# A second double unit with seven block products, sums shared with GpSimd, and another opening list

## The chip, the cores and the metric

The kernel runs on one core of a Trainium2 chip. The metric is the device time of one execution in microseconds. TensorE (PE in the profile) multiplies, VectorE (DVE), ScalarE (ACT) and GpSimd (POOL) work on elements, SyncE (SP) only issues DMAs here, and POOL issues DMAs too.

## What is computed

The reference is a chunked attention followed by a two-layer block with a residual. Cut to what matters:

```python
# attention: 4 batches, 8 heads, 768 rows, 64 columns; 8 memory rows
for c in range(24):                       # chunks of 32 rows
    k_full = concat([mem_k, k[l_start:r_end]])   # 16 rows to the left, 8 to the right
    v_full = concat([mem_v, v[l_start:r_end]])
    scores = 0.125 * q_c @ k_full.T
    a = exp(scores - max(scores)); a = a / sum(a)
    out[c] = a @ v_full
# second block: x is out with the heads side by side, (4, 768, 512)
xn = (x - mean(x)) / sqrt(var(x) + 1e-6) * g_ln
out = x + relu(xn @ w_ch1) @ w_ch2        # 512 -> 2048 -> 512
```

Matmuls are in 16-bit floats with 32-bit sums; DMAs issued by POOL convert the 32-bit inputs on the way.

## The kernel before, in words

**Tiles.** The 3,072 rows are 24 token tiles t of 128 rows, six to a batch; two tiles make a unit u (0 to 11) of 256 rows. For a token tile: `qk_products` (L311) makes scores in one PSUM bank, `row_max` and `less_max` subtract the maximum on DVE, `weights` takes the exponential on ACT, `pt_products` and `pt_copy` turn the weights, `val_products` (L366) multiplies with V into the bank pair `two`, `tokens` (L380) divides and makes the negative mean on DVE, `shift` (L393) subtracts the mean on POOL or ACT, `x_products` and `x_copy` turn the tile and scale it by g, and `square` and `root_of` (L414, on POOL) make the reciprocal of the deviation, which `add_to` (L648) applies at the end.

**Up and down.** For units 0 to 9, `up_products(u, s, bank)` (L460) makes step s of 8 (256 of 2,048 hidden columns) with 8 matmuls 128x128 by 128x256, and `relu_up` evicts the bank. Down, for units 1 to 11, is a two-by-two block product (token halves by hidden halves by column halves) with seven products in place of eight, `down7_products(u, part, bank)` (L659), parts 0 to 6 of 8 matmuls each. Parts 2 to 6 add onto the bank of an earlier part, so an `add_to` on DVE must have read that bank first. The left sides of parts 2 to 5 are sums of relu blocks, `r_sum(u, k)` (L626, instruction at L637), k from 0 to 3: sum 1 uses sum 0, and sum 3 uses sum 1. A whole sum is 128x1024; with `lo, hi` it is made in halves of 128x512.

**Up with seven products.** Units 10 and 11 are one double unit: up is there a two-by-two block product too, of rows (unit 10, unit 11), x halves and hidden halves. `up7_products(c, k, bank, add)` (L558, matmuls at L578) makes product k (1 to 7) of a quarter c (0 to 3) with 4 matmuls. It needs sums of W1 blocks, `w1_sum(k, n, d, engine)` (L531, L542; 16 pieces of 128x512), and of x blocks, `x_sum(k, engine)` (L547, L554), called XS0 to XS3; XS1 uses XS0 and XS3 uses XS1. In one bank the products 1, 6, 5 and 3 are added up: after each of the first three, `hold` (L592) copies the bank to 32-bit floats on ACT, and after the last `relu_sum` evicts it on ACT. Products 2, 7 and 4 go to other banks, and `relu_of_sum` (L595, L596) on DVE adds a held copy and takes the relu.

**Banks.** Six PSUM banks are shared by all products: `one[0..1]`, `upb[0..1]`, `dnb[0..1]`.

**The order** is written out by hand, and each engine works through its own instructions in that order. There are three stretches. L707 to L1083 is the opening list: loads, units 0 to 2 and the attention of token tiles 0 to 9. From L1085 a plan spreads loads, attention and sums over 16 steps of each unit 3 to 7, between `up(u, step)` and `down7(u - 1, part)`. From L1149 on comes the tail, a list of units 8 to 11, down of unit 7 and the attention of tiles 18 to 23.

**The opening list.** POOL issues the loads in the order of the list: first two loads each of k, q, v of batch 0 in its first part and the same for its second part (12 loads, 2,304 KB in 16-bit), then `load_w1(0)`, `(2)`, `(1)`, `(3)` and `load_w2(0..3)` (512 KB each, L164, L169), with loads of batch 1 (`load_octets`, `load_v_group`) between. w1 chunk n holds the hidden columns of up steps 2n and 2n+1. The V tiles need ones behind each head: L713 writes them on DVE for both tiles at once. `mix` (L266) reorders loaded rows for the turns `turn_whole`, on DVE, ACT or POOL. The up steps of unit 0 come in the order 0, 5, 2, 4, 1, 3, 7, 6 (L841 on).

Of the kernel before, what the change touches and what calls it, by code (L numbers as in the profile page):

```python
# [18 lines left out]
def kernel(  # L19
# [31 lines left out]
    zeros = sb.tile([128, 512], FP16, name="zeros")  # L51
    mhalf = sb.tile([128, 1], FP32, name="mhalf")
# [443 lines left out]
    def down_add(t, p):  # L496
# [8 lines left out]
    flat_q = QD[0].rearrange("p j s -> p (j s)")  # L505
    RS_two = [
# [6 lines left out]
    rT_last = [  # L513
        raw[2][o].rearrange("p j r d -> p (j r d)").rearrange("p (n c) -> p n c", c=256)
        for o in range(2)
    ]
# [4 lines left out]
    XS = [P[0].rearrange("p (d c) -> p d c", d=2), P[1].rearrange("p (d c) -> p d c", d=2)] + [  # L521
        PT[i].rearrange("p j q -> p (j q)").rearrange("p (d c) -> p d c", d=2) for i in range(2)
# [5 lines left out]
    def r_totals(u):  # L528
        return RS_two if u == NP - 2 else RS
# [14 lines left out]
    def x_block(i, j):  # L544
        return xT[(NP - 2 + j) % 3][:, 2 * i : 2 * i + 2, :]

    def x_sum(k, engine):  # L547
        a, b = (
            (x_block(0, 1), x_block(0, 0)),
            (x_block(1, 1), XS[0]),  # L550
            (x_block(1, 1), x_block(0, 1)),
            (x_block(1, 0), XS[1]),
        )[k]
        on(engine).tensor_tensor(  # L554
            out=XS[k], in0=a, in1=b, op=ALU.subtract
        )

    def up7_products(c, k, p, add):  # L558
# [7 lines left out]
        def total(m):  # L566
# [6 lines left out]
            (block(0, 0), x_block(0, 0)), (block(1, 0), x_block(1, 0)), (total(3), x_block(1, 1)),  # L573
# [10 lines left out]
    def r_part(j, o, c):  # L584
        if j == 0:
            return rT[(NP - 2) % 2][:, 8 * o + 2 * c : 8 * o + 2 * c + 2, :]
        return rT_last[o][:, 2 * c : 2 * c + 2, :]
# [4 lines left out]
    def hold(p, e):  # L592
        nc.scalar.copy(out=e, in_=p)

    def relu_of_sum(j, o, c, p, e):  # L595
        nc.vector._custom_dve(  # L596
            TENSOR_ADD_SAT, out=r_part(j, o, c), in0=pair(p), in1=pair(e), s0=TOP, s1=0.0,
        )

    def relu_sum(c, p):  # L600
        nc.scalar.activation(out=r_part(1, 0, c), in_=pair(p), func=ACTF.Relu)
# [19 lines left out]
    def r_block(u, i, o):  # L621
        if u == NP - 1:
            return rT_last[o][:, :, 128 * i : 128 * i + 128]
        return rT[u % 2][:, 8 * o : 8 * o + 8, 128 * i : 128 * i + 128]

    def r_sum(u, k, lo=0, hi=8):  # L626
# [10 lines left out]
        nc.vector.tensor_tensor(  # L637
# [59 lines left out]

    VT = KT[1]
# [13 lines left out]
    for i in range(2):  # L712
        nc.vector.memset(V[i][:, :, :, 64:VW], 1.0)  # L713
        nc.vector.memset(V[i][0:16, 0, :, 64:VW] if i == 0 else V[i][0:16, 0, :, :], 0.0)
        nc.vector.memset(V[i][96:128, NG - 1, :, :], 0.0)
    nc.vector.memset(memv16[:, :, :, 64:VW], 1.0)
# [5 lines left out]
    copy_on("A")(out=mem16, in_=mem32)  # L722
    load_octets(0, 0, k, 0, 0, 48, (0,))
    load_octets(0, 0, k, 0, 0, 48, (1,))
    make_identity(nc, identity)
    mem_products(upb[1])
    warm(6, one[0])
    tk1 = turn(raw[0][0], 1, 48, one[0])
    load_octets(1, 0, q, 0, 0, 32, (1,))
    mem_copy(upb[1], "A")  # L730
    load_octets(1, 0, q, 0, 0, 32, (0,))
    mem_cols(VT, memT[:, 16:20, :], "V")
    tk0 = turn(raw[0][0], 0, 48, upb[0])
    warm(1, one[1])
    tq1 = turn(raw[1][0], 1, 32, one[1])
    to_rows(0, tq1, 1, "A", 32, 0, 16, 32)
    mem_cols(KT[0], memT[:, 0:4, :], "A")
    tq0 = turn(raw[1][0], 0, 32, dnb[1])
    to_rows(0, tq0, 0, "A", 32, 0, 16, 32)
    to_stream(KT[0], tk1, 1, "V", 48, 0)  # L740
    load_octets(2, 0, v, 0, 0, 48, (0,))
    to_stream(KT[0], tk0, 0, "V", 48, 0)
    warm(4, dnb[0])
    s1 = qk_products(1, dnb[0])
    to_rows(0, tq0, 0, "A", 32, 0, 0, 16)
# [12 lines left out]
    s0 = qk_products(0, upb[0])
    load_octets(2, 1, v, 0, 48, 48, (0,))
    load_octets(1, 1, q, 0, 32, 64, (1,))  # L760
    mix_into(whole[2], raw[2][1], 0, 96, "V")
    tV0 = turn_whole(whole[2], 0, 96, dnb[1])
    v1 = v_products(1, one[1])
    row_max(0, s0)
    less_max(0, s0)
    v_copy(1, v1, "V")
    v3 = v_products(3, upb[1])
    v0 = v_products(0, one[0])
    less_max(1, s1)
    v_copy(0, v0, "V")  # L770
    load_octets(0, 1, k, 0, 48, 48, (0,))
    load_octets(0, 1, k, 0, 48, 48, (1,))
    mix_into(whole[1], raw[0][1], 0, 96, "V")
    to_stream(VT, tV0, 0, "A", 48, 48)
    v_copy(3, v3, "A")
    v2 = v_products(2, upb[0])
    load_octets(1, 1, q, 0, 32, 64, (0,))
    load_w1(0)
    load_w1(2)
    load_w1(1)  # L780
    weights(0)
    load_w1(3)
    p0 = pt_products(0, dnb[1])
    weights(1)
    pt_copy(0, p0, "V")
    v_copy(2, v2, "V")
    p1 = pt_products(1, one[1])
    mix_into(whole[2], raw[2][1], 1, 96, "A")
    load_w2(0)
    val_products(0)  # L790
    tokens(0)
    mix_into(whole[3], raw[1][1], 1, 128, "A")
    tV1 = turn_whole(whole[2], 1, 96, upb[1])
    to_stream(VT, tV1, 1, "A", 48, 48)
    mix_into(whole[3], raw[1][1], 0, 128, "P")
    load_w2(1)
    tQ0 = turn_whole(whole[3], 0, 128, dnb[0])
# [4 lines left out]
    tQ1 = turn_whole(whole[3], 1, 128, one[0])  # L802
    to_rows(0, tQ0, 0, "A", 64, 32)
    pt_copy(1, p1, "V")
    val_products(1)
    load_octets(0, 0, k, 1, 0, 48, (0,))
    copy_on("V")(
# [3 lines left out]
    to_rows(0, tQ1, 1, "A", 64, 32)  # L811
    mix_into(whole[1], raw[0][1], 1, 96, "V")
    tK1 = turn_whole(whole[1], 1, 96, dnb[1])
    tokens(1)
    shift(0, "P")
    x0 = x_products(0, upb[0])
    x_copy(0, x0)
    to_stream(KT[0], tK1, 1, "V", 48, 48)
    shift(1, "A")
    tK0 = turn_whole(whole[1], 0, 96, one[1])  # L820
    to_stream(KT[0], tK0, 0, "A", 48, 48)
    load_octets(0, 0, k, 1, 0, 48, (1,))
    square(0)
    x1 = x_products(1, upb[1])
    load_v_group(1, 9, 1)
    x_copy(1, x1)
    v6 = v_products(6, dnb[0])
    v5 = v_products(5, one[0])
    square(1)
    v_copy(5, v5, "V")  # L830
    root_of(0)
    v4 = v_products(4, upb[0])
    v_copy(4, v4, "V")
    load_w2(2)
    load_w2(3)
    v10 = v_products(10, dnb[1])
    v_copy(10, v10, "V")
    s2 = qk_products(2, one[1])
    row_max(2, s2)
    load_mem_rows(1, B)  # L840
    up_products(0, 0, upb[1])  # L841
    relu_up(0, 0, upb[1], "V")
    up_products(0, 5, one[0])
    relu_up(0, 5, one[0], "A")
    load_v_group(1, 8, 1)
    less_max(2, s2)
    weights(2)
    load_v_group(1, 7, 1)
    load_octets(1, 0, q, 1, 0, 48, (0,))
    up_products(0, 2, upb[0])  # L850
    relu_up(0, 2, upb[0], "A")
    up_products(0, 4, dnb[1])
    relu_up(0, 4, dnb[1], "A")
    p2 = pt_products(2, upb[1])
    pt_copy(2, p2, "V")
    up_products(0, 1, one[1])
    relu_up(0, 1, one[1], "A")
    load_octets(0, 1, k, 1, 48, 48, (1,))
    v7 = v_products(7, one[0])
    v_copy(7, v7, "A")  # L860
    s3 = qk_products(3, upb[0])
    row_max(3, s3)
    less_max(3, s3)
    v8 = v_products(8, dnb[1])
    load_octets(0, 1, k, 1, 48, 48, (0,))
    v9 = v_products(9, upb[1])
    v_copy(9, v9, "A")
    val_products(2)
    tokens(2)
    shift(2, "P")  # L870
    mix(0, 0, "P")
    up_products(0, 3, one[1])
    relu_up(0, 3, one[1], "V")
    load_v_group(1, 1, 0)
    v_copy(6, v6, "V")
    w2_sum(0)
    weights(3)
    up_products(0, 7, one[0])
    up_products(0, 6, upb[1])
    relu_up(0, 6, upb[1], "A")  # L880
    load_octets(1, 0, q, 1, 0, 48, (1,))
    down_products(0, 0, upb[0])
    down_products(0, 1, upb[0])
    p3 = pt_products(3, one[1])
    down_products(1, 0, dnb[0])
# [576 lines left out]
```

## Time and profile before

| what | value |
|---|---|
| median of 3 runs | 224.45 us (224.44 to 224.99) |
| the profiled execution's own time | 224.56 us |
| its span, first to last instruction | 222.8 us |
| mean granted TensorE clock | 0.992 |
| bytes moved by DMA | 23.24 MB |

The profile's time is counted from the start of the span. "L637" is a line of the kernel. A line of a timeline gives the start, the duration, the engine, the line, the operation, out<-in and the form; in square brackets stand idle time of the engine just before it and what ended it. PEld is the weight load, which runs beside PE. A matmul is pipelined, so its shown duration overlaps the next one's.

### The profile page before, as it was taken

What the parts mean: (1) busy time and instruction counts of PE and PEld (TensorE: products, weight loads), DVE (VectorE), ACT (ScalarE), POOL (GpSimd) and SP (SyncE); (2) the same over time, 40 slices, a digit from 0 to 9 for tenths busy, and PEclk for the clock granted to TensorE, in tenths of its full rate; (3) what the DMA queues carried; (4) which work ended last, traced back from release to release, by engine and by line L of the source; (5) the groups of instructions that cost most, each with busy time, mean ns of one, the idle gap of its engine ahead of it and who ended that gap; (6) DMA issues with size and microseconds to landing.
All of it is one profiled execution on the core that took longest, in us unless ns stands there. A gap on an engine that the chain in (4) does not pass through costs nothing.

```text
span 222.8 us, 8324 instructions
## 1 busy us (share of the span) xinstructions
PE 213.6 (96%) x3578; PEld 188.3 (84%) x3578; DVE 178.3 (80%) x396; ACT 132.0 (59%) x260; POOL 128.2 (58%) x203
## 2 busy tenths in 40 slices
PE   6977999998999999999999999999999999999993
PEld 2456895698999989999999999999898999999982
DVE  6587956897898987896686996895789987788983
ACT  3297766677786388468447278378757743654100
POOL 7937327888989726976454937415277548930000
PEclk9996999999999999999999999999999999999999
DMA  4999999999984993994952992952100011101115
GB/s 76 183 191 207 213 205 208 189 136 133 137 52 57 206 162 68 130 74 113 157 73 57 144 131 59 107 98 63 50 3 3 3 47 50 47 4 49 47 56 184
DMA packets 43450, 23.24 MB, mean 104 GB/s; under 512 B 30004, under 2 KB 39796, under 8 KB 43364
## 3 DMA queue, kind: packets, MB, share of 16 engines
q0 software_dynamic: 38416, 14.48, 56.8%
q1 hardware_dynamic: 4996, 8.22, 12.7%
q8 instruction: 28, 0.46, 0.8%
q14 instruction: 10, 0.08, 0.1%
HBM read 29.02 MB, written 6.29 MB: 158 GB/s over the span
## 4 chain that ended last, share of the span: by engine, by line
PE 85%; DMA 4%; POOL 4%; DVE 3%; issue 1%; ACT 1%; DVEq 0%; POOLq 0%
PE upb L464 22%; PE dnb L643 20%; PE one L464 6%; PE one L643 5%; DMA raw<-in_q_dram 4%; PE upb L643 4%; PE two L373 4%; PE one L274 3%; POOL raw L107 3%; PE dnb L464 2%; PE dnb L578 2%; PE one L578 2%; PE one L429 2%; PE one L322 2%; PE dnb L490 2%; PE upb L490 2%
## 5 line engine op out<-in xcount | busy, mean ns | idle before, releaser
L464 PEld LDWEIGHTS <-w1c 128*128 128x128 f16 x640 | 67.4, 114 | 1.7
L464 PE MATMUL upb<-xT,w1c 128*128 128x256 f16 x448 | 58.3, 273 | 0.0
L456 ACT ACTIVATE rT<-upb 128x512 f16<-128x512 f32 x53 | 30.9, 595 | 17.6 <-PE upb L464 17.6
L650 DVE SCALAR_TENSOR_TENSOR xs<-dnb,rstd,xs 128x256 f32<-128x256 f32 x54 | 25.9, 479 | 11.3 <-PE dnb L643 9.5
L643 PEld LDWEIGHTS <-RS 128*128 128x128 f16 x320 | 30.4, 98 | 3.2
L344 ACT ACTIVATE P<-sub 128x512 f16<-128x512 f32 x24 | 15.0, 633 | 25.0 <-DVE sub L334 25.0
L416 POOL TENSOR_SCALAR veps<-ssq 128x1 f32<-128x1 f32 x24 | 5.6, 235 | 36.9 <-ACT sq L409 36.1
L643 PEld LDWEIGHTS <-rT 128*128 128x128 f16 x240 | 22.9, 98 | 2.3
L643 PE MATMUL dnb<-T,RS 128*128 128x256 f16 x184 | 23.9, 273 | 0.0
L396 POOL TENSOR_SCALAR xn<-xs,nmean 128x512 f16<-128x512 f32 x18 | 13.8, 768 | 14.8 <-DVE nmean L389 11.5
L637 DVE TENSOR_TENSOR RS<-rT 128x1024 f16<-128x1024 f16 x18 | 13.5, 754 | 5.4 <-ACT rT L456 5.4
L464 PE MATMUL one<-xT,w1c 128*128 128x256 f16 x136 | 17.4, 273 | 0.0
L409 ACT ACTIVATE sq<-xs,nmean 128x512 f16<-128x512 f32 x24 | 17.3, 720 | 0.1
L383 DVE CUSTOM_DVE_ANT_1 xs<-two,rec 128x512 f32<-128x512 f32 x24 | 16.6, 691 | 0.8
L420 POOL TENSOR_TENSOR rstd<-veps,mhalf 128x1 f32<-128x1 f32 x24 | 13.5, 563 | 2.0
L643 PE MATMUL dnb<-w2c,rT 128*128 128x256 f16 x112 | 14.4, 272 | 0.0
L116 POOL DMA_DIRECT2D V<-in_v_dram x16 | 13.6, 848 | 0.7 <-PE dnb L643 0.6
L456 ACT ACTIVATE rT<-one 128x512 f16<-128x512 f32 x15 | 9.1, 606 | 5.8 <-PE one L464 5.7
L445 DVE TENSOR_TENSOR xT<-one,g_col 128x512 f16<-128x512 f16 x14 | 9.6, 686 | 3.6 <-PE one L429 3.4
L249 ACT COPY QD<-one 128x768 f16<-128x768 f16 (+2 forms) x12 | 9.4, 784 | 5.0 <-PE one L228 4.1
L274 PEld LDWEIGHTS <-raw 96*128 96x128 f16 x192 | 10.5, 98 | 1.5 <-issue 1.2
L373 PEld LDWEIGHTS <-PT 64*32 64x32 f16 x768 | 7.4, 94 | 5.0 <-issue 3.3
(192 smaller groups left out, 479.6 us busy)
## 6 DMA issues: line engine op xcount, KB each, us to landing
out_dram<-xs SPq DMA_DIRECT2D x23, 256.0 KB, 2.1
raw<-in_k_dram POOLq DMA_DIRECT2D x16, 192.0 KB, 6.6
raw<-in_q_dram POOLq DMA_DIRECT2D x12, 192.0 KB, 7.1
w1c<-in_moe_w_ch_dram POOLq DMA_DIRECT2D x4, 512.0 KB, 13.4
w2c<-in_moe_w_ch_dram POOLq DMA_DIRECT2D x4, 512.0 KB, 14.5
V<-in_v_dram POOLq DMA_DIRECT2D x16, 77.0 KB, 3.8
raw<-in_v_dram POOLq DMA_DIRECT2D x4, 192.0 KB, 5.7
V<-memv SPq DMA_DIRECT2D x6, 120.0 KB
```

The lines of the kernel that those rows point to most:

```text
L116: nc.gpsimd.dma_start(out=V[b % 2][72:128, 0 : NG - 1, h, 0:64], in_=dram(v, base + 16 * D, [[64, 56], [64 * 64, NG - 1], [1, 64]]),)
L274: nc.tensor.matmul(out=pv[:, rows * r : rows * r + rows], lhsT=m[0:rows, jj, r, :], rhs=identity[0:rows, 0:rows], is_transpose=True, start ...
L344: nc.scalar.activation(out=P[t % 3], in_=sub[t % 2], func=ACTF.Exp, scale=0.125)
L373: nc.tensor.matmul(out=two[col : col + 32, 128 * h : 128 * h + 65], lhsT=PT[t % 3][rows, 2 * (h // 4) + h % 2, q0 : q0 + 32], rhs=V[b % 2] ...
L383: nc.vector.tensor_tensor_reduce(out=x.rearrange("p (h d) -> p h d", h=H), in0=free(two, 0, [[128, 8], [1, 64]]), in1=free(r, 0, [[1, 8], ...
L396: nc.gpsimd.tensor_scalar(out=xn[i], in0=x, scalar1=m, scalar2=1.0, op0=ALU.add, op1=ALU.mult,)
L409: nc.scalar.activation(out=sq, in_=xs[t % 9], func=ACTF.Square, bias=nmean[t % 6], scale=1.0, accum_out=ssq[i],)
L420: nc.gpsimd.tensor_tensor(out=rstd[t % 9], in0=veps[i], in1=mhalf, op=ALU.pow)
L456: nc.scalar.activation(out=o, in_=i, func=ACTF.Relu)
L464: nc.tensor.matmul(out=p[:, 256 * hb : 256 * hb + 256], lhsT=free(w1c[hc // 4][:, dt, :], hc % 4, [[4, 128]]), rhs=xT[u % 3][:, dt, :], st ...
L643: nc.tensor.matmul(out=p[:, 0:256], lhsT=left[:, n, :], rhs=right(n), start=(n == 0 and not add), stop=(n == 7), skip_group_check=add,)
L650: nc.vector.scalar_tensor_tensor(out=x, in0=p[:, 0:256], scalar=rstd[t % 9], in1=x, op0=ALU.mult, op1=ALU.add,)
```

## The change

1. Units 8 and 9 become a double unit as well: `up7_products`, `x_sum`, `relu_of_sum` and `relu_sum` take the unit as an argument, and in the tail 28 calls of `up7_products` take the place of the 16 `up_products` of units 8 and 9. A new tile `spare` holds the x sums and one of the two sets of held copies, since the tiles used so far are still in use then.
2. `r_sum` takes an engine. In the tail 21 r sum instructions go to POOL (whole: sums 1 and 3 of unit 7, 1 and 2 of unit 9; halves: most of units 8, 10 and 11), 11 stay on DVE. The whole tail has a new order.
3. Eight of the 16 W1 sum pieces move to the plan, on POOL, in units 6 and 7; of the eight left in the tail, seven are on POOL.
4. The opening list is replaced by an older one.

The new helper code, cut to its core:

```diff
+    spare = sb.tile([128, 5120], FP16, name="spare")
...
-        [flat_q[:, 1024 * i : 1024 * i + 1024].bitcast(FP32) for i in range(3)],
+        [spare[:, 1024 * i : 1024 * i + 1024].bitcast(FP32) for i in range(3)],
...
-        return RS_two if u == NP - 2 else RS
+        return RS_two if u in (NP - 4, NP - 2) else RS
...
-    def x_block(i, j):
-        return xT[(NP - 2 + j) % 3][:, 2 * i : 2 * i + 2, :]
+    def x_block(u, i, j):
+        return xT[(u + j) % 3][:, 2 * i : 2 * i + 2, :]
...
-    def r_sum(u, k, lo=0, hi=8):
+    def r_sum(u, k, lo=0, hi=8, engine="V"):
...
-        nc.vector.tensor_tensor(
+        on(engine).tensor_tensor(
...
+    def ready_v(i, eng):
+        eng.memset(V[i][:, :, :, 64:VW], 1.0)
+        eng.memset(V[i][0:16, 0, :, :], 0.0)
+        eng.memset(V[i][96:128, NG - 1, :, :], 0.0)
+        eng.tensor_copy(
+            out=V[i][96:128, NG - 1, :, 64:VW],
+            in_=free(last[96:128, 0:1], 0, [[0, H], [0, VW - 64]]),
+        )
...
+    slots = ((6, 13), (6, 14), (6, 15), (7, 5), (7, 6), (7, 7), (7, 9), (7, 10))
+    pieces = ("000", "001", "100", "101", "200", "201", "300", "301")
+    for (u, step), piece in zip(slots, pieces):
+        at(u, step, w1_sum, *map(int, piece), "P")
```

The older opening list, at the places that matter (lines between are left out). It has the 12 loads of batch 0 in another order, then these calls, of which only loads, POOL work and up steps are shown up to the first turns of batch 1:

```python
    load_w1(0)
    nc.gpsimd.memset(V[0][:, 4:NG, :, 64:VW], 1.0)
    load_octets(1, 0, q, 1, 0, 48, (0,))
    load_v_group(1, 11, 1)
    load_w1(3)
    load_w1(1)
    load_octets(1, 0, q, 1, 0, 48, (1,))
    mix_into(whole[2], raw[2][1], 0, 96, "P")
    load_w2(0)
    load_w1(2)
    mix_into(whole[1], raw[0][1], 1, 96, "P")
    shift(1, "P")
    load_w2(1)
    load_w2(2)
    load_w2(3)
    load_octets(0, 0, k, 1, 0, 48, (0,))
    mix(1, 0, "P")
    root_of(0)
    load_octets(0, 0, k, 1, 0, 48, (1,))
    up_products(0, 1, upb[1])
    up_products(0, 0, upb[0])
    up_products(0, 2, one[0])
    up_products(0, 6, dnb[0])
...
    ready_v(1, nc.gpsimd)
    root_of(2)
    load_octets(1, 1, q, 1, 48, 48, (0,))
    nc.gpsimd.memset(memv16[:, :, :, 64:VW], 1.0)
...
    shift(4, "P")
    load_octets(0, 1, k, 1, 48, 48, (0,))
...
    mix(0, 1, "P")
    lk10 = turn_whole(mixed[0], 0, 96, dnb[0])
```

The new tail, at the places that matter:

```python
    down7_products(7, 1, one[1])
    r_sum(7, 0, 0, 8, "V")
    tokens(18)
    r_sum(7, 2, 0, 8, "V")
    r_sum(7, 1, 0, 8, "P")
    down7_products(7, 2, upb[1])
    r_sum(7, 3, 0, 8, "P")
    add_to(14, 1, upb[1])
    down7_products(7, 4, upb[1])
...
    x_sum(8, 2, "P")
    x_sum(8, 1, "V")
    up7_products(8, 0, 6, dnb[1], True)
...
    r_sum(9, 2, 0, 8, "P")
    r_sum(8, 0, 0, 4, "P")
    x_sum(10, 2, "P")
    x_sum(10, 0, "V")
    x_sum(10, 1, "V")
    up7_products(10, 1, 6, dnb[0], True)
...
    r_sum(10, 0, 4, 8, "V")
    r_sum(11, 0, 4, 8, "P")
    r_sum(11, 1, 4, 8, "P")
    r_sum(10, 1, 4, 8, "V")
    r_sum(10, 3, 4, 8, "V")
    down7_products(10, 2, dnb[0])
    r_sum(11, 3, 4, 8, "P")
    down7_products(10, 4, dnb[0])
    r_sum(11, 2, 4, 8, "P")
    r_sum(11, 3, 0, 4, "P")
    down7_products(11, 6, upb[1])
    add_to(23, 0, upb[1])
    store(23, 0, 256)
```

In the list before, the last instructions are `add_to(22, 1, ...)`, `store(21)` and `store(22)`.

More of the change, by code (lines that the diff above doesn't have):

```diff
@@ L556, in x_sum, with up7_products @@
         )
[L558 removed]
+    def up7_products(u, c, k, p, add):
         def block(i, o):
@@ L785 @@
[L785 to L797, printed above, removed]
+    load_octets(2, 0, v, 0, 0, 48, (1,))
+    to_stream(KT[0], tk0, 0, "V", 48, 0)
@@ L810 @@
     )
[L811 to L826, printed above, removed]
@@ L847 @@
[L847 to L861, printed above, removed]
+    load_v_group(1, 6, 1)
+    up_products(0, 7, upb[1])
@@ new lines @@
+    down7_products(1, 1, dnb[1])
+    down7_products(1, 2, dnb[0])
+    add_to(2, 0, dnb[1])
+    square(5)
+    square(6)
+    shift(6, "A")
+    less_max(8, s8)
+    s9 = qk_products(9, upb[1])
+    row_max(9, s9)
+    weights(8)
+    val_products(7)
+    load_v_group(1, 10, 0)
+    tokens(7)
+    load_v_group(1, 11, 0)
+    down7_products(1, 5, one[1])
+    up_products(2, 3, dnb[1])
+    store(1)
+    up_products(2, 7, upb[0])
+    add_to(2, 1, dnb[0])
+    down7_products(1, 4, dnb[0])
+    relu_up(2, 0, one[0], "A")
@@ new lines @@
+    down7_products(7, 3, one[1])
+    tokens(19)
+    shift(19, "A")
+    add_to(14, 1, upb[1])
+    down7_products(7, 4, upb[1])
+    w1_sum(2, 1, 0, "P")
+    square(19)
+    row_max(21, s21)
+    add_to(15, 1, one[1])
+    root_of(19)
+    x19 = x_products(19, one[0])
+    x_copy(19, x19, "A")
+    less_max(21, s21)
+    hold(dnb[0], held[1][0])
+    x_sum(8, 0, "P")
+    add_to(15, 1, upb[1])
+    down7_products(7, 5, one[1])
+    up7_products(8, 0, 1, dnb[1], False)
+    hold(dnb[1], held[0][0])
@@ new lines @@
+    shift(20, "P")
+    x20 = x_products(20, upb[0])
+    w1_sum(3, 1, 1, "P")
+    w1_sum(3, 1, 0, "P")
+    hold(one[1], held[1][2])
+    up7_products(8, 3, 3, one[1], True)
+    hold(dnb[1], held[0][2])
+    relu_of_sum(8, 1, 1, 2, upb[1], held[0][2])
+    up7_products(8, 2, 3, dnb[1], True)
+    up7_products(8, 3, 7, dnb[0], False)
+    pt_copy(23, p23, "A")
+    relu_sum(8, 3, one[1])
+    relu_of_sum(8, 1, 1, 3, dnb[0], held[1][2])
+    shift(21, "P")
+    x21 = x_products(21, one[0])
+    shift(22, "P")
@@ new lines @@
+    down7_products(9, 3, upb[0])
+    x_copy(22, x22, "A")
+    shift(23, "A")
+    r_sum(8, 1, 0, 4, "P")
+    down7_products(9, 1, one[1])
+    r_sum(8, 2, 4, 8, "P")
+    add_to(18, 0, one[1])
+    x23 = x_products(23, upb[1])
+    down7_products(9, 2, dnb[1])
+    x_copy(21, x21, "A")
+    x_copy(23, x23, "V")
+    x_sum(10, 2, "P")
+    x_sum(10, 0, "V")
+    x_sum(10, 1, "V")
+    up7_products(10, 1, 1, dnb[0], False)
+    up7_products(10, 3, 1, one[0], False)
+    r_sum(8, 0, 4, 8, "P")
@@ new lines @@
+    r_sum(8, 1, 4, 8, "P")
+    up7_products(10, 0, 1, one[1], False)
+    add_to(18, 1, dnb[1])
+    up7_products(10, 1, 2, upb[1], False)
+    hold(dnb[0], held[1][0])
+    up7_products(10, 1, 6, dnb[0], True)
+    relu_of_sum(10, 0, 0, 1, upb[1], held[1][0])
+    hold(one[1], held[0][0])
+    hold(dnb[0], held[1][1])
+    down7_products(9, 4, dnb[1])
+    square(20)
+    up7_products(10, 0, 6, one[1], True)
+    hold(one[1], held[0][1])
+    up7_products(10, 1, 5, dnb[0], True)
+    add_to(19, 1, upb[0])
@@ new lines @@
+    add_to(19, 1, dnb[1])
+    r_sum(9, 3, 0, 8, "V")
+    down7_products(9, 6, dnb[1])
+    add_to(19, 0, dnb[1])
+    up7_products(10, 0, 5, one[1], True)
+    hold(dnb[0], held[1][2])
+    up7_products(10, 1, 3, dnb[0], True)
+    relu_sum(10, 1, dnb[0])
+    hold(one[0], held[1][0])
+    down7_products(9, 5, upb[0])
+    down7_products(8, 0, upb[1])
+    x_sum(10, 3, "V")
+    add_to(18, 1, upb[0])
+    store(18)
+    r_sum(8, 3, 0, 4, "V")
+    up7_products(10, 1, 7, dnb[1], False)
+    hold(one[1], held[0][2])
@@ new lines @@
+    r_sum(11, 0, 0, 4, "P")
+    root_of(20)
+    add_to(17, 1, one[1])
+    down7_products(8, 4, upb[1])
+    add_to(17, 1, upb[1])
+    hold(one[0], held[1][2])
+    up7_products(10, 3, 3, one[0], True)
+    relu_sum(10, 3, one[0])
+    up7_products(10, 2, 2, dnb[0], False)
+    store(19)
+    root_of(22)
+    relu_of_sum(10, 0, 1, 0, upb[0], held[0][1])
+    r_sum(10, 0, 0, 4, "P")
+    r_sum(10, 1, 0, 4, "P")
+    up7_products(10, 2, 6, dnb[1], True)
+    hold(dnb[1], held[0][1])
+    down7_products(8, 6, upb[1])
```

1055 lines of the change are left out of this document (484 added, 571 removed).

## The prediction

> **What bounds the kernel now.** I read the page first, then the busy time by stretch, then each engine's timeline in the opening list and in the tail.
>
> ```profile
> span 222.8 us, 8324 instructions
> ...
> PE 213.6 (96%) x3578; PEld 188.3 (84%) x3578; DVE 178.3 (80%) x396; ACT 132.0 (59%) x260; POOL 128.2 (58%) x203
> ...
> PE   6977999998999999999999999999999999999993
> ```
>
> TensorE is the bound from the eighth slice on. The stretches that I chose end where the work changes: the first up projection (24.88), the first instruction after the planned units (156.05), the last matmul's end (219.3).
>
> ```profile
> 24.88:62.00 37.12, 36.36 (x694) 30.34 (x685) 28.90 (x62) 25.57 (x52) 27.67 (x44) 1.00 1.27 170
> 62.00:156.05 94.05, 93.84 (x1616) 86.79 (x1614) 76.60 (x174) 60.44 (x113) 57.53 (x96) 1.00 0.80 103
> 156.05:219.30 63.25, 63.21 (x884) 58.28 (x881) 54.12 (x116) 30.53 (x68) 27.21 (x32) 1.00 0.11 38
> 219.30:222.80 3.50, 0.00 (x0) 0.00 (x0) 0.48 (x1) 0.00 (x0) 0.00 (x0) 1.00 0.46 171
> ```
>
> Columns: length, then busy time of PE, PEld, DVE, ACT and POOL, clock, DMA. In the tail TensorE has 0.04 us free of 63.25, DVE is busy 86% and POOL 43%. So a matmul removed there is time removed, as long as nothing else comes late; and what delays TensorE anywhere after 24.88 is added in full. The profiled execution took 224.56 us (222.8 of span and 1.8 around it), 0.11 above the median of 224.45; my sum is made against 224.56.
>
> **Part 1, fewer matmuls.** Sixteen `up_products` of 8 matmuls (128) become 28 `up7_products` of 4 (112). In the tail's timeline eight matmuls follow each other in 0.87 us, four in 0.44, so 109 ns each: 16 x 0.109 = **-1.74 us**, on the path. The price is evictions. The 16 relus (14 on ACT, 2 on DVE) go; 12 holds and 4 relus come on ACT (0.59 and 0.60 us each), 12 sums with relu on DVE (0.68), 4 more x sums (0.42 on DVE, 1.16 on POOL). DVE would get 12 x 0.68 - 2 x 0.68 = 6.8 us more, which is why the r sums go to POOL.
>
> **Part 2, sums on GpSimd.** Before, 28 r sums of the tail are on DVE; after, 11 are, and 21 instructions go to POOL: 4 of 128x1024 and 17 of 128x512 (some are former whole sums cut in two). POOL's 128x512 sums take 1.15 to 1.30 us (w1_sum rows), the 128x1024 form isn't in the trace: between 1.16 (no dearer than the half) and 2.6 (two of the dearest), and I take 2.3, two halves. POOL's tail then holds 17 x 1.16 + 4 x 2.3 + 7 w1 sums and 4 x sums x 1.16 + about 7 for shifts and roots = 49 us of some 62, up from 27. What this does to DVE stands in these rows:
>
> ```profile
> 174.65 0.47 DVE L650 SCALAR_TENSOR_TENSOR xs<-one,rstd,xs 128x256 f32<-128x256 f32 x1
> 175.04 1.64 DVE L637 TENSOR_TENSOR RS<-RS,rT 128x1024 f16<-128x1024 f16 x1
> ...
> 184.88 1.48 DVE L637 TENSOR_TENSOR RS<-rT,RS 128x1024 f16<-128x1024 f16 x1
> ```
>
> ```profile
> 174.98 1.16 POOL L542 TENSOR_TENSOR raw<-raw,w1c 128x512 f16<-128x512 f16 x1
> ...
> 184.65 1.16 POOL L554 TENSOR_TENSOR P<-xT,P 128x512 f16<-128x512 f16 x1 [1.36 <-DVE P L554]
> 185.89 1.49 POOL L554 TENSOR_TENSOR PT<-xT,P 128x512 f16<-128x512 f16 x1
> ```
>
> A clean r sum is 0.68. Beside a POOL sum that began first it ends 0.54 us after POOL's end (176.14 and 176.68; 185.81 and 186.36), so it stood still until POOL was done, and the next POOL sum is late in turn (1.49). The add_to of 0.47 and the relu of sum (0.68 to 0.69 in every row) show no such wait. After the change 16 DVE instructions in the tail (11 r sums, 4 x sums, 1 w1 sum) meet a POOL that sums or shifts 80% of the time.
>
> I followed the new list by hand with these durations, each eviction 0.15 us behind its matmuls. It loses: about 0.5 where down part 4 of unit 7 waits for an add_to that stands behind r_sum(7,2) on DVE, itself held by r_sum(7,1) on POOL; 0.35 at the first product with XS1, whose sum stands behind the x sum on POOL; 0.6 where both x sums of unit 10 on DVE meet r_sum(9,2) on POOL; and some 1.4 at the end, where three half sums of unit 10 on DVE alternate with five of unit 11 on POOL and down parts 2 and 4 of unit 10 wait. That is 2.85; between these places the banks come free in time. Hand-followed waits are partly absorbed by the next one, so I take **+1.6 us**, and 0 to 3.3 as bounds: 0 if every wait has cover, as in the tail now, 3.3 if none has. With part 1 the tail is then level: 63.1 instead of 63.25.
>
> The Trainium skill bears on one term (SBUF — State Buffer, section "Who interferes with whom"): a VectorE instruction with two SBUF inputs and a GpSimd one that reads SBUF exclude each other for the whole instruction. The rows agree for 1.16 us of POOL; no row shows a longer one. By that page a whole r sum on POOL would hold DVE up to an estimated 2.3 us, and the four would cost an estimated 1 us more than if DVE came in after 1.2.
>
> **Part 3, W1 sums from unit 6.** Eight go into the planned units, all on POOL, 8 x 1.16 = 9.3 us in two units of some 18 us where POOL is at 61%. Queued behind one there are shift (needed by x_products five steps later, more than 5 us), root, and the last DMA issues of batch 3. Held DVE sums there (at most 1.1 us each) feed down parts several steps later: **0**, at most 0.5. Without that cover one shift late by 1.16 would stall x_products by as much.
>
> **Part 4, the older opening list.** Its matmuls are the same but for 3 more warm ones while TensorE waits for data anyway. Two things differ on the path. First, the DMA order.
>
> ```profile
> 25.48 1.20 POOL L171 DMA_DIRECT2D w2c<-in_moe_w_ch_dram  x2
> 29.13 0.70 POOL L181 DMA_DIRECT2D memv<-in_mem_v_dram  x1 [2.45 <-DMA w1c<-in_moe_w_ch_dram]
> 31.13 0.59 POOL L146 DMA_DIRECT2D V<-in_v_dram  x1 [1.29 <-DMA w2c<-in_moe_w_ch_dram]
> ```
>
> The 24th load that POOL issues (memv) waits for a w1 chunk, the 16th; the 25th waits for the 17th (w2). So each issue waits for the eighth before it, and the waits date the landings: the 12th (last q of batch 0) at 17.7, where POOL's mix of it starts, and the 16th at 29.1. Between them lie 2,048 KB: 179 KB per us. Now w1(1) is third of the w1 chunks, 3,840 KB from the start, landed at about 26.2; up step 2, which needs it, starts at 26.65. In the older list 192 KB of q and a V group of 32 KB precede it: 26.2 + 224/179 = 27.4 us.
>
> ```profile
> 24.88 1.06 PE L464 MATMUL upb<-xT,w1c 128*128 128x256 f16 x8
> 25.77 1.04 PE L464 MATMUL one<-xT,w1c 128*128 128x256 f16 x8
> 26.65 1.04 PE L464 MATMUL upb<-xT,w1c 128*128 128x256 f16 x8
> 27.52 1.04 PE L464 MATMUL dnb<-xT,w1c 128*128 128x256 f16 x8
> ```
>
> By 27.5 three up steps are done now. In the older list its third step in TensorE's order is step 2, which can't start before 27.4; only two are done by then, and one V turn more (0.24): 0.87 - 0.24 = 0.63 us late, even if the two steps themselves come early, as by hand they do (first step at 24.2). Second, POOL. It gets memsets of the V ones (1,536 columns took DVE 1.34 us, off the path, at 1.5 to 5.1; POOL's 128 columns took 0.22, so some 3.5 us of POOL for the later ones). Behind them stand root, the loads of batch 1, shift of token tile 4 and the last k load of batch 1, then mix(0,1) on POOL (2.0 us) which lk10 on TensorE needs. By hand k is issued at 47.6, lands in 6.6 us (median), and lk10 waits about 1.2 us; shift costs 0.2. The list before has one such stall, 0.88 at 51.36 (a turn of q: half its matmuls at 51.36, the rest at 52.40), which goes. So 0.63 + 1.4 - 0.9 = **+1.2 us**; bounds 0 (POOL in time, w1 faster) and 3 (both in full and the stall kept).
>
> **Part 5, the end.** Last store: 128 KB behind the last add instead of 256 KB. DMA moved 171 GB/s there, so at most 0.13 MB/171 = 0.77 us; half a store is only one part of the 3.0 us from the last add to the end: **-0.3**, from -0.7 to 0.
>
> **Sum:** -1.74 + 1.6 + 0 + 1.2 - 0.3 = +0.76; 224.56 + 0.76 = **225.3 us**. 0.3% is 0.67 us, about what a measurement of this kernel can tell from no change.
>
> **Rivals.**
> - *The tail keeps up* (gaps 0.3 instead of 1.6): for it, the tail now runs at 86% DVE with several held sums and no gap. Against, these sums had slack of several parts, while XS1 and the end have none. -1.74 + 0.3 + 0.6 to 1.2 - 0.3 = 223.4 to 224.0; with an opening that costs nothing 222.8. Chance 0.30, all faster by over 0.3%, or at its edge.
> - *The opening costs nothing* while the tail pays 1.6: 224.56 - 0.44 = 224.1. For it, first up step early; against, w1(1)'s place in the queue. Chance 0.16, within 0.3%.
> - *The port makes DVE the bound of the tail*, the other side. Its work there becomes 54.1 - 3.4 (held time in the rows now) - 9.2 (r sums moved) + 6.8 (part 1) + 1.3 (three x sums) - 1.9 (two w1 sums, an x copy, a PT copy) = 47.7 us; TensorE's is 61.5. So it decides from 13.8 us of held time in 16 waits, 0.86 each. At 17 us (1.06 each, most of a POOL half sum) the tail takes 64.7, 1.45 over now: 224.56 + 1.45 + 1.2 - 0.3 = 226.9. Chance 0.20. For it, POOL at 80%; against, POOL waits too and leaves openings.
> - *Forecast*, 224.5 to 226.2: 0.34, a quarter of it within 0.3%.
>
> Faster 0.30, within 0.3% 0.24, slower 0.46. Range 222.9 to 227.2: from the keeping tail with a free opening to the bound DVE.
>
> **What would show it.** Opening: PE's third up step at 27.4 or later and POOL's mix ahead of a stalled lk10 near 54. Tail: DVE two-input sums above 0.68 (0.42 for halves) beside POOL sums, POOL's whole sums near 2.3, and gaps of PE at the places named. Wrong if the new tail from its first matmul to its last takes under 62 or over 65 us, or if the planned units start earlier than now (71.7, the up products behind the last down part of unit 1).

## The result and the profile after

The changed kernel takes 226.95 us (226.50 to 228.22, 4 runs) against 224.49 us (224.44 to 224.99, 4 runs) for the kernel before on the same chip: ratio 1.0121, 95% interval 1.0095 to 1.0147, so 2.46 us slower. The forecast was 225.3, slower by 0.8. The profiled execution took 226.50 us with a span of 224.7, against 224.56 and 222.8 before; it is the fastest of the four, so some 0.5 us of the 2.46 are in no profile. The ratios in this document leave out executions more than 1.5% above the fastest of their kernel (one of 231.06 us in experiment 2, one of 226.89 us of the kernel before).

The page of the changed kernel, its first lines and the row of TensorE by fortieths of the span:

```profile
span 224.7 us, 8335 instructions
...
PE 210.8 (94%) x3565; PEld 184.4 (82%) x3565; DVE 178.3 (79%) x380; ACT 137.0 (61%) x271; POOL 163.4 (73%) x232
...
PE   6777999999999999999999999989999999999891
```

TensorE is busy 2.8 us less, DVE exactly as long as before, POOL 35 us more. (In the tail 5.7 us of DVE's time is waiting inside two-input instructions, added up from their rows over the durations of 0.42 and 0.68 us without a wait; the prediction counts 3.4 before.) Behind the opening two slices that were 9 now read 8: the 27th (146 to 152 us), and the 38th (208 to 213).

The busy times by stretch, after: from the first up step to 62 us, then the planned units, the tail up to the last matmul's end, the end (columns as in the prediction's block).

```profile
24.09:62.00 37.91, 37.23 (x704) 31.17 (x694) 29.69 (x62) 27.43 (x57) 30.82 (x49) 1.00 1.17 168
62.00:156.68 94.68, 93.29 (x1599) 85.51 (x1597) 78.35 (x173) 59.57 (x111) 65.38 (x101) 1.00 0.81 103
156.68:220.20 63.52, 62.23 (x868) 56.33 (x865) 53.97 (x107) 34.77 (x77) 48.23 (x47) 1.00 0.09 31
220.20:224.70 4.50, 0.01 (x1) 0.00 (x0) 0.53 (x2) 0.00 (x0) 0.00 (x0) 0.78 0.64 231
```

With the start of unit 3 (its first up step) as a further mark, and the same rule for the last matmul's end in both, the two spans divide like this:

| stretch | before | after | difference | predicted |
|---|---|---|---|---|
| start to first up step of unit 3 | 71.69 | 71.06 | -0.63 | +1.2 |
| units 3 to 7, to the tail's first instruction | 84.36 | 85.62 | +1.26 | 0 |
| tail, to the last matmul's end | 63.2 | 63.5 | +0.3 | -0.14 |
| last matmul's end to the end of the span | 3.56 | 4.52 | +0.96 | -0.3 |
| span | 222.8 | 224.7 | +1.9 | +0.76 |

So the tail, where the change is, came out nearly level. What was lost lies before it and after it. The first row alone is no finding: in the profiles of ten kernels with the older list that mark lies between 70.4 and 72.1 us (experiment 5). The other three rows add up to 2.5 us, about the measured difference.

**Planned units.** Here are DVE, POOL and the waiting TensorE in the timeline of the changed kernel:

```profile
137.72 1.24 DVE L212 COPY KT<-memT 128x64 f16<-128x64 f16 x1
137.74 1.17 POOL L548 TENSOR_TENSOR raw<-w1c 128x512 f16<-128x512 f16 x1
...
139.53 1.17 POOL L548 TENSOR_TENSOR raw<-w1c 128x512 f16<-128x512 f16 x1
139.67 1.59 DVE L643 TENSOR_TENSOR RS<-RS,rT 128x1024 f16<-128x1024 f16 x1
...
145.51 1.15 POOL L548 TENSOR_TENSOR raw<-raw,w1c 128x512 f16<-128x512 f16 x1
145.92 1.28 DVE L643 TENSOR_TENSOR RS<-rT,RS 128x1024 f16<-128x1024 f16 x1
...
151.34 0.38 PE L354 MATMUL one<-identity,P 128*128 128x128 f16 x4 [0.62 <-DVE sub L335]
...
151.93 0.50 PE L275 MATMUL one<-identity,raw 96*128 96x96 f16 x8 [0.21 <-DVE xT L446]
```

The same DVE instructions in the kernel before, with one that shows idle time:

```profile
138.47 0.16 DVE L211 COPY KT<-memT 128x64 f16<-128x64 f16 x1
139.56 0.69 DVE L637 TENSOR_TENSOR RS<-rT 128x1024 f16<-128x1024 f16 x1 [0.85 <-ACT rT L456]
140.28 0.69 DVE L637 TENSOR_TENSOR RS<-RS,rT 128x1024 f16<-128x1024 f16 x1
...
145.89 0.68 DVE L637 TENSOR_TENSOR RS<-rT,RS 128x1024 f16<-128x1024 f16 x1
```

Three DVE instructions stand beside a W1 sum of POOL and take 1.24, 1.59 and 1.28 us; without one they take 0.16, 0.69 and 0.68. That is 2.6 us. From 139 to 152 DVE goes from one instruction to the next, so the delay travels to the end of its queue: to the subtraction of a maximum (L335) and an xT copy (L446) that have nothing to do with the sums, and there TensorE waits. The waits of 0.62 and 0.21 us stand at the same two instructions, equal to 0.01, in experiments 3, 4, 7, 8 and 9, which have these sums at the same places. The Trainium skill (SBUF — State Buffer, section "Who interferes with whom") names both kinds of victim: VectorE instructions with two SBUF inputs, and also copies in a mode that takes both ports. The copy of 64 columns held for 1.24 us agrees, if it runs in such a mode, which the trace doesn't show.

**The end of the tail.** DVE, POOL and TensorE, changed kernel:

```profile
207.91 1.30 DVE L643 TENSOR_TENSOR V<-V,rT 128x512 f16<-128x512 f16 x1
...
209.00 1.21 POOL L643 TENSOR_TENSOR RS<-RS,QD 128x512 f16<-128x512 f16 x1
...
211.60 1.30 DVE L643 TENSOR_TENSOR RS<-RS,QD 128x512 f16<-128x512 f16 x1
211.73 1.03 PE L649 MATMUL dnb<-T,V 128*128 128x256 f16 x8 [0.68 <-DVE xs L656]
...
213.93 1.03 PE L649 MATMUL dnb<-T,rT 128*128 128x256 f16 x8 [0.30 <-DVE xs L656]
```

Half sums of 0.42 us take 1.19 (at 209.31, not shown) to 1.30 on DVE, in turn with POOL's, and TensorE waits at down parts 4 and 6 of unit 10 for adds that stand behind them. The distances between matmul starts put the two gaps at 0.84 and 0.46 us (longer than the idle time in brackets, as a matmul's shown duration runs on beside the next one's start).

**The end.** Busy times of single microseconds behind 220, changed kernel; the last column is what DMA moved, in GB/s:

```profile
220.00:221.00 1.00, 0.21 (x2) 0.00 (x0) 0.73 (x2) 0.00 (x0) 0.00 (x0) 1.00 1.03 363
221.00:222.00 1.00, 0.00 (x0) 0.00 (x0) 0.00 (x0) 0.00 (x0) 0.00 (x0) 1.00 1.04 383
222.00:223.00 1.00, 0.00 (x0) 0.00 (x0) 0.00 (x0) 0.00 (x0) 0.00 (x0) 0.86 0.97 349
```

DMA is full for three microseconds. The last six stores (tiles 16, 23 high, 20, 22, 21, 23 low: four of 256 KB, two of 128 KB, 1.28 MB) all go out behind 218.6. Before, transfers began at 216, and no whole microsecond fills the engines; this is the fullest one:

```profile
220.00:221.00 1.00, 0.00 (x0) 0.00 (x0) 0.00 (x0) 0.00 (x0) 0.00 (x0) 1.00 0.83 309
```

From the last add's end to the end of the span it is now 4.0 us, before 3.0.

### The profile page after: what moved, and what is told of

It is laid out like the page before. It is cut to its first block, busy times and chain, and to the rows that moved or that the text cites. A ratio compares the mean times of both kernels' runs of the same rounds, so it can differ in the third digit from the quotient of the medians.

```text
span 224.7 us, 8335 instructions
## 1 busy us (share of the span) xinstructions
PE 210.8 (94%) x3565; PEld 184.4 (82%) x3565; DVE 178.3 (79%) x380; ACT 137.0 (61%) x271; POOL 163.4 (73%) x232
## 4 chain that ended last, share of the span: by engine, by line
PE 65%; DMA 13%; DVE 12%; POOL 3%; issue 2%; ACT 2%; SPq 1%; DVEq 0%; ACTq 0%; POOLq 0%
PE dnb L649 15%; PE upb L465 14%; DMA w1c<-in_moe_w_ch_dram 5%; PE dnb L584 5%; PE upb L649 4%; PE one L649 4%; DVE xs L656 3%; DMA raw<-in_q_dram 3%; DMA V<-memv 3%; PE one L584 3%; PE two L374 3%; PE upb L584 2%; PE one L275 2%; DVE RS L643 2%; POOL raw L108 2%
## 5 line engine op out<-in xcount | busy, mean ns | idle before, releaser
L465 PEld LDWEIGHTS <-w1c 128*128 128x128 f16 x512 | 53.6, 114 | 2.0 <-DMA w1c<-in_moe_w_ch_dram 0.6
L465 PE MATMUL upb<-xT,w1c 128*128 128x256 f16 x400 | 51.9, 273 | 0.3 <-ACT rT L457 0.3
L649 PEld LDWEIGHTS <-RS 128*128 128x128 f16 x288 | 27.4, 98 | 3.1 <-issue 0.3
L649 PE MATMUL dnb<-T,RS 128*128 128x256 f16 x152 | 19.7, 273 | 0.0
L397 POOL TENSOR_SCALAR xn<-xs,nmean 128x512 f16<-128x512 f32 x15 | 10.4, 696 | 9.8 <-DVE nmean L390 6.0
L584 PEld LDWEIGHTS <-raw 128*128 128x128 f16 x128 | 13.7, 114 | 0.6 <-DVE spare L560 0.5
L643 DVE TENSOR_TENSOR RS<-rT 128x1024 f16<-128x1024 f16 x14 | 9.8, 700 | 4.7 <-ACT rT L457 4.5
L242 DVE COPY KT<-one 128x192 f16<-128x192 f16 (+1 forms) x20 | 10.1, 548 | 1.5 <-PE one L229 0.9
L362 ACT COPY PT<-one 128x512 f16<-128x512 f16 x15 | 8.8, 586 | 4.1 <-PE one L354 3.3
L108 POOL DMA_DIRECT2D raw<-in_k_dram x16 | 9.9, 620 | 1.7 <-POOLq L1489 0.8
```

The costliest lines, as they stand in the source:

```text
L108: nc.gpsimd.dma_start(out=raw[i][half][par : 2 * n : 2], in_=dram(src, (b * H + par) * HS + 512 * lo, [[512, n], [2 * HS, 4], [1, 512]]),)
L465: nc.tensor.matmul(out=p[:, 256 * hb : 256 * hb + 256], lhsT=free(w1c[hc // 4][:, dt, :], hc % 4, [[4, 128]]), rhs=xT[u % 3][:, dt, :], st ...
L584: nc.tensor.matmul(out=p[:, 256 * hb : 256 * hb + 256], lhsT=left(hb, d), rhs=right[:, d, :], start=(not add and hb == 0 and d == 0), stop ...
L643: on(engine).tensor_tensor(out=R[k][:, lo:hi, :], in0=a[:, lo:hi, :], in1=b[:, lo:hi, :], op=op)
L649: nc.tensor.matmul(out=p[:, 0:256], lhsT=left[:, n, :], rhs=right(n), start=(n == 0 and not add), stop=(n == 7), skip_group_check=add,)
```

## The experiments

The theory behind them: (a) the planned units lose 1.2 us because sums on POOL hold DVE, and DVE's queue carries the delay on; (b) the tail's gain is eaten at its end by the same exclusion; (c) the end loses 1 us to stores sent together; (d) the older opening costs nothing. The rival for (a) and (b) is that DVE is short of time whoever makes the sums; for (c) that the last store's own latency sets the end; for (d) my predicted +1.2. Each run is compared with the kernel before on its own chip and at its own hour (medians of 224.27 to 224.61 us there), and its profile is divided into the same stretches. The changed kernel wasn't measured again beside them: a time against it is the difference of two ratios and carries about +-0.9 us, so the finer argument rests on the profiles, one for each kernel.

**1. Without the W1 sums in the plan** (a; the eight pieces aren't made, their tiles are only filled once with zeros)

```diff
-        at(u, step, w1_sum, *map(int, piece), "P")
```

> The changed kernel without the eight W1 sum pieces in units 6 and 7 (they are left out, so the up products of units 8 to 11 use wrong sums; three short memsets in the idle start keep their rows defined). Theory: beside these POOL sums DVE's r sums, and a copy of the memory columns, stand still, 2.6 us in all, scores come late and TensorE waits. Then the planned units (first up of unit 3 to the first down part of unit 7) take 84.4 us as before the change, not 85.6, DVE's r sums there are back at 0.68, and the time falls by 1.0 to 1.4 us. Rival: the planned units are longer because the other opening list leaves the engines in another phase; then they stay at 85.6 and the time falls by less than 0.3.

226.05 us (12 runs), ratio 1.0068 (1.0041 to 1.0096). Against the changed kernel's 1.0121 that is 1.2 us less, as expected. All waits between 147.5 and 152 are gone:

```profile
151.08 0.39 PE L354 MATMUL one<-identity,P 128*128 128x128 f16 x4
```

From an up step before this instruction to the turn behind it the changed kernel takes 4.45 us (147.48 to 151.93), and this one 3.10 (148.21 to 151.31), as before the change. The whole planned stretch is 85.14, only 0.48 shorter and not the 84.4 expected, as two stalls of some 0.5 us appear at 84 and 114 us. The profile gives no releaser for them ("issue"); another run has one at the same place near 84, the others have none. They are not explained.

**2. The same sums at other steps** (a)

```diff
-    slots = ((6, 13), (6, 14), (6, 15), (7, 5), (7, 6), (7, 7), (7, 9), (7, 10))
+    slots = ((6, 7), (6, 9), (6, 13), (6, 14), (6, 10), (6, 11), (7, 9), (7, 10))
```

> The changed kernel with the same eight pieces on POOL, but six of them in steps 7 to 14 of unit 6 and two in steps 9 and 10 of unit 7, so that none runs beside the r sums of steps 0 to 5 of unit 7. Theory of the shared access: POOL's work is the same, yet the planned units shrink to 84.4 to 84.8 us and the time by 0.8 to 1.3. Rival, POOL itself is the bound there (shifts and loads late behind its sums): the planned units stay within 0.3 of 85.6, since POOL has the same work.

229.06 us (6 runs from 227.20 to 231.06), 1.0172 (1.0126 to 1.0218): slower still, which neither the theory nor the rival expected. The planned stretch takes 87.06 in the profile, which is of the fastest execution; what the others lost beyond it no profile shows. The sums meet other instructions, copies too, earlier in the same DVE queue:

```profile
135.60 1.34 POOL L548 TENSOR_TENSOR raw<-w1c,w1c 128x512 f16<-128x512 f16 x1
135.84 1.37 DVE L262 COPY raw<-raw 96x1024 f16<-96x1024 f16 x1
...
139.93 2.73 DVE L643 TENSOR_TENSOR RS<-RS,rT 128x1024 f16<-128x1024 f16 x1
```

The longest wait of TensorE comes by way of ACT, whose exponential waits for the late subtraction on DVE and holds up the relu behind it:

```profile
147.39 0.63 ACT L345 ACTIVATE P<-sub 128x512 f16<-128x512 f32 x1 [5.42 <-DVE sub L335]
...
148.56 1.03 PE L465 MATMUL upb<-xT,w1c 128*128 128x256 f16 x8 [0.74 <-ACT rT L457]
```

Here moving POOL's work along the queue only changed who is held. (Why one sum takes 2.73 us, when POOL's sum beside it begins 0.6 later and takes 1.17, stays open; POOL issues loads right before and after that sum.)

**3. One store earlier** (c)

```diff
     down7_products(8, 5, one[1])
     r_sum(10, 3, 4, 8, "V")
+    add_to(16, 1, one[1])
+    store(16)
```

(taken away further down)

> The changed kernel with the last add of tile 16 and its store moved up from the last four down parts to right behind the down part that it belongs to, some 8 us earlier. Theory: at the end six stores, 1.25 MB, drain at about 380 GB/s and the last one waits for the others; with 256 KB out of the way the end after the last add falls from 4.0 to about 3.3 us and the time by 0.5 to 0.8. Rival: the last store has a fixed time of its own, or DMA is as late with five stores: the end stays at 3.8 to 4.0 and the time within 0.3.

226.89 us, 1.0100 (1.0068 to 1.0131); the end takes 4.31 instead of 4.52. From the last add's end it is 3.8 us, against 4.0 and an expected 3.3, so the expectation failed: five stores of 1 MB are still sent behind the last adds, and DMA moves 343 and 381 GB/s in the two microseconds behind the last matmul. It left (c) and its rival both standing; run 8 tells them apart.

**4. The opening list of before in the changed kernel** (d)

> The changed kernel with the opening list of before; plan and tail are those of the change. Theory from the two profiles: the older list lets the planned units begin 0.63 us earlier, so this one starts them at 71.7 and is 0.4 to 0.8 us slower. Rival: the profile of before had a stretch of half TensorE clock at 18.9 to 22.3 us that the other had not, and the lists are equal without it: within 0.3. My forecast of a loss by the older list would make it 1.2 us faster.

227.47 us, 1.0121 (1.0087 to 1.0155); unit 3 starts at 71.95 instead of 71.06, the planned units take 85.92 instead of 85.62, tail and end are as in the changed kernel. The profile is as the theory has it, but the ratio is that of the changed kernel to the last digit: by time the expected loss of 0.4 to 0.8 us is not shown, and +-0.9 can't exclude it.

**5. The older opening list in the kernel before** (d)

> The kernel before with only the list of units 0 to 2 put in from the changed kernel; planned units, tail and end as before. Theory (the older opening is the faster one: 71.06 us to the first up step of unit 3 against 71.69): that step at 70.4 to 71.9, mean of the other three profiles with this list 71.0, planned units 84.4, tail 63.2, end 3.5, and the time 0.4 to 0.9 us under before. Rival, my predicted +1.2 from the late W1 chunk and the late mix: that step at 72.9, the time about 1 us over before. Second rival (the two lists are level and profiles differ by chance): within 0.3 us of before.

224.36 us (12 runs), 0.9995 (0.9975 to 1.0016). In its profile unit 3 starts at 70.83; in all ten profiles with this list that start lies between 70.4 and 72.1, mean 71.2, and in the two with the newer one at 71.7 and 71.95. By time the lists are level within 0.25%, as the second rival has it; the +1.2 is excluded, and whether 0.5 us is gained can't be told.

**6. The plan's sums on DVE** (a; the engine `"P"` becomes `"V"`)

> The changed kernel with the eight W1 sums of units 6 and 7 on VectorE instead of GpSimd, in the same slots. Theory (the stretch loses 1.16 us because sums of 1.16 us on GpSimd shut out VectorE's two-input operations): each costs 0.42 us on VectorE and shuts nothing out, so the jump of 1.2 us between 148.5 and 152 falls to under 0.4, the planned units to 84.4 to 84.9 and the time by 0.8 to 1.2 against the changed kernel. Rival (VectorE simply has no room for more work there, 8 x 0.42 = 3.4 us): the jump stays at 1 us or more.

226.88 us (6 runs), 1.0114 (1.0084 to 1.0145); planned stretch 85.26. No DVE instruction is held any more, each piece takes 0.42 us, but only a third of the loss is gone in the profile, and by time no gain is shown (0.2 us, where 0.8 to 1.2 was expected):

```profile
147.07 0.75 DVE L548 TENSOR_TENSOR raw<-w1c,w1c 128x512 f16<-128x512 f16 x2
...
150.63 0.38 PE L354 MATMUL one<-identity,P 128*128 128x128 f16 x4 [0.45 <-DVE sub L335]
```

Three pieces (1.1 us; one at 145.41, and these two) stand inside the same unbroken stretch of DVE work. So the rival is half right: what counts is any time put into that stretch, held or worked. Behind it, at 152, DVE has idle time again.

**7. The five half sums of unit 11 on DVE** (b)

```diff
-    r_sum(11, 0, 4, 8, "P")
+    r_sum(11, 0, 4, 8, "V")
...
```

> The changed kernel with the five half sums of unit 11 at the end (11,0; 11,1; 11,3 twice; 11,2) on VectorE instead of GpSimd, places in the list unchanged. Theory (three half sums of unit 10 on VectorE take 1.2 to 1.3 us each because they alternate with GpSimd's, and the adds behind them free the banks late): VectorE does all of them in 0.42 us each, the gaps of 0.84 us at down part 4 and 0.46 at down part 6 of unit 10 go for the most part, the tail takes 62.2 to 62.7 instead of 63.5, the time falls by 0.8 to 1.3 against the changed kernel. Rival (the end is short of VectorE time, and GpSimd's help is needed): gaps as large or larger, the time no better.

226.98 us (6 runs), 1.0109 (1.0084 to 1.0135); tail 63.53, no gain, as the rival has it. But the gaps named did shrink, by 0.64 and 0.46 us; all DVE half sums are at 0.41 to 0.43. A new wait of 1.1 takes their place:

```profile
217.61 0.88 DVE L656 SCALAR_TENSOR_TENSOR xs<-one,rstd,xs 128x256 f32<-128x256 f32 x2 [0.46 <-PE one L649]
218.40 0.41 DVE L643 TENSOR_TENSOR RS<-QD 128x512 f16<-128x512 f16 x1
...
218.87 0.61 PE L649 MATMUL upb<-T,RS 128*128 128x256 f16 x4 [0.94 <-DVE RS L643]
```

On POOL the last two sums ran ahead, as nothing stood in POOL's queue; in DVE's they stand behind adds that wait for TensorE, and TensorE waits for the sums.

**8. Three stores sent when their tiles are done** (c)

```diff
     add_to(22, 0, upb[0])
+    add_to(21, 0, dnb[0])
+    store(21)
+    add_to(16, 1, one[1])
+    store(16)
...
     add_to(20, 1, dnb[1])
+    store(20)
```

(each taken away further down)

> The changed kernel with three of its last six stores sent when their tiles are done: the last add of token tile 21 and its store and those of tile 16 move up behind down part 6 of unit 10, the store of tile 20 behind its last add. Theory (1.28 MB of stores wait in one queue and drain at 350 to 380 GB/s behind the last matmul): 0.77 MB leaves before, the stretch from the last matmul to the end of the span falls from 4.5 to 3.4 to 3.8, and the time by 0.7 to 1.0 against the changed kernel. Rival (what follows the last add is the last store's own latency, as moving the one store of tile 16 alone seemed to say, 4.3): it stays at 4.2 to 4.5.

225.54 us (12 runs), 1.0058 (1.0041 to 1.0075), 1.4 us under the changed kernel, more than expected.

```profile
span 223.8 us, 8336 instructions
...
220.63 0.48 DVE L656 SCALAR_TENSOR_TENSOR xs<-upb,rstd,xs 128x256 f32<-128x256 f32 x1 [0.39 <-PE upb L649]
```

The end takes 3.23 us, 1.3 less than in the changed kernel; planned units and tail are the same to 0.01. From the last add's end it is 2.7 us: the half store as the last one is worth 0.3 against the 3.0 of before, as forecast, once nothing stands in front of it.

**9. Runs 7 and 8 together, the two late sums moved up** (b, c)

```diff
...
+    r_sum(11, 2, 4, 8, "V")
+    r_sum(11, 3, 0, 4, "V")
     add_to(21, 0, dnb[0])
...
```

> The changed kernel with the stores spread as in the run before and the five half sums of unit 11 on VectorE, the two that were queued too late there (0.94 us of wait at 218.9) now right behind the half sum of (10,3), where VectorE has 1.2 us free. Theory (the gaps of 0.84 and 0.46 us at down parts 4 and 6 of unit 10 come from VectorE and GpSimd taking turns, and the 0.94 us came only from the place in the queue): tail 62.3 to 62.7 instead of 63.5, end 3.2 to 3.5, planned units still 85.6, and the time 1.8 to 2.4 under the changed kernel, so about level with the kernel before. Rival (VectorE has no room at the end for what GpSimd took): the gap moves again, the tail stays at 63.3 or more.

224.72 us (12 runs), 1.0012 (0.9989 to 1.0035): level with the kernel before. Tail 62.40, end 3.24. (Its planned stretch, 86.05, has one of the unexplained stalls, at 85.)

**10. And the plan's sums on DVE, behind the full stretch** (a, b, c)

```diff
+    slots = ((6, 13), (6, 14), (6, 15), (7, 9), (7, 10), (7, 12), (7, 13), (7, 14))
...
+        at(u, step, w1_sum, *map(int, piece), "V")
```

> As the run above, and the eight W1 sums of the planned units on VectorE, five of them moved from steps 5 to 10 of unit 7 to its steps 9 to 14, where VectorE is idle for 2 us. Theory (in the run with them on VectorE the 0.8 us that were left came from the 1.5 us of sums that stood inside the chain of VectorE work between 139.5 and 151): planned units 84.4 to 84.8 instead of 85.6, and with tail 62.5 and end 3.3 a time 2.6 to 3.4 under the changed kernel, 0.2 to 1.0 under the kernel before. Rival (other VectorE work is late there too): planned units 85.2 or more, level with the kernel before at best.

223.00 us (12 runs), 0.9935 (0.9910 to 0.9960), faster than both kernels: 1.5 us under the kernel before, where 0.2 to 1.0 was expected. Its planned units, tail and end in busy times:

```profile
71.48:155.74 84.26, 84.03 (x1456) 77.63 (x1456) 70.11 (x162) 52.65 (x97) 47.26 (x78) 1.00 0.83 105
155.74:218.20 62.46, 62.09 (x868) 56.39 (x865) 53.16 (x112) 34.81 (x77) 42.48 (x42) 1.00 0.11 42
218.20:221.50 3.30, 0.00 (x1) 0.00 (x0) 0.48 (x1) 0.00 (x0) 0.00 (x0) 0.81 0.36 127
```

The planned units are back at 84.3, the tail is at 62.4 and the end at 3.3. Three of the tail's gaps are left, by the distances between matmul starts: 0.26 us at down part 4 of unit 7, 0.38 at the product with XS1 of unit 10 and 0.2 at down part 4 of unit 10.

## Why the prediction was wrong

Slower was right, by a third of the size, and the parts that make it slower are other ones than forecast. That makes the sign luck: without the +1.2 of part 4, which didn't happen, the same sum gives -0.44. It is luck too that 226.95 lies inside the range: its upper part belonged to the rival that DVE becomes the bound, which didn't happen either.

- **Part 1, fewer matmuls, and part 2, sums on GpSimd: the mechanism was right, the sizes nearly.** Forecast -1.74 and +1.6 of gaps. Measured gaps: 0.26 at down part 4 of unit 7 (0.5 by hand), nothing at XS1 of unit 8 (0.35), 0.38 at XS1 of unit 10 (0.6), 0.84 and 0.46 at the end (1.4 by hand): 1.94 in all. Without them the tail is 63.5 - 1.94 = 61.6, and the tail of before less the forecast is 63.2 - 1.74 = 61.5, so the products do give what was counted for them. At XS1 of unit 10 the sum took 1.27 us beside a half sum of unit 8 on POOL, the next one behind r_sum(9,2):

```profile
187.27 0.63 PE L584 MATMUL dnb<-spare,raw 128*128 128x256 f16 x4 [0.22 <-DVE spare L560]
```

  A whole r sum on POOL takes 2.12 to 2.45 us, as taken. The rule that the prediction took from the Trainium skill (SBUF — State Buffer, section "Who interferes with whom"), and by which the four whole sums would cost an estimated 1 us more, can't be judged here: no DVE sum met one in its first part; the one that met its last 0.3 us (159.83) ended 0.55 behind it.
- **Part 3, W1 sums in the plan: the first failed step, 0 forecast, +1.26 measured.** "Held DVE sums there (at most 1.1 us each) feed down parts several steps later: 0" looked only at who reads the held sum. What became late was everything behind it in DVE's queue. The windows show the cover: from 137 to 148 us DVE was busy 9.65 us of 11 before, and 10.77 after. Three held instructions of 2.6 us against 1.35 of idle time leave about 1.2, and the stretch came out 1.26 longer. The 9.3 us of POOL that I weighed show no wait of their own: behind the start of unit 3, the waits of TensorE in the planned units that the profile puts above 0.1 us all name DVE. With the same sums on DVE, behind the full stretch, the planned units are back at 84.3 (run 10).
- **Part 4, the opening: not there, +1.2 forecast, -0.63 in the two profiles, -0.1 (+-0.5) by time.** Both its stalls failed, and the sign that the prediction set against itself, planned units that start earlier than 71.7, came true; with a spread of 70.4 to 72.1 it was too fine a sign. The chunk w1(1) "landed at about 26.2" plus 224 KB at 179 KB per us, 27.4; in the changed kernel the third up step starts at 26.37, after 0.34 us of waiting for that chunk:

```profile
26.37 1.07 PE L465 MATMUL one<-xT,w1c 128*128 128x256 f16 x8 [0.34 <-DMA w1c<-in_moe_w_ch_dram]
```

  A mean rate over two waits far apart, plus a landing that itself was extrapolated, was off by 1.0 us, more than the 0.63 it was to show. And POOL was in time: mix(0,1) ends at 53.64, and lk10 starts at 54.32 behind an up step, without a wait.
- **Part 5, the end: the second failed step, -0.3 forecast, +0.96 measured,** is counting the last store alone ("Last store: 128 KB behind the last add instead of 256 KB"). The list also sends the stores of tiles 16, 20, 21 and 22 between 218.6 and 221.0 us, together with both halves of tile 23. The half store's own 0.3 was right (run 8).
- **Rivals.** What "the opening costs nothing" supposed happened, though not its time of 224.1. "The port makes DVE the bound" did not happen in the tail: 5.7 us of held time there, where 13.8 would have decided. The exclusion did cost in the planned units, which no rival had.

## What to carry to other kernels

When an instruction gets longer, follow the whole queue of its engine to the next idle time, not only the reader of its result: the cost is the added time minus the idle time up to the first instruction that a bound engine waits for. A sum moved to a helper engine (here 1.16 us in place of 0.42) is only free if it doesn't exclude the engine it came from; and moved back, its place in the queue must be found again, because a queue that ran ahead doesn't any more. At the end, add up all the bytes that are stored behind the last few results, not the last store's alone.

## What the runs showed of the hardware beyond that

- A copy of 128x64 elements on VectorE, 0.16 us alone, took 1.24 beside a GpSimd sum: the exclusion is not limited to two-input instructions.
- Stores from one queue of SyncE move up to 383 GB/s when they stand behind each other, where the slices of the opening that are full of loads move 193 to 214 (page of the changed kernel).
- The granted TensorE clock is halved for 3.4 us in the opening in some executions (before, runs 1 and 9) and in others not, with the same instructions. In run 1 the first up step came at 24.96 instead of 24.09, yet unit 3 no later (70.86); where that was made up wasn't followed.
